# Norm statistics of two blocks on ScalarE, one head group moved forward, and the second GLU chunk's weights read and split early

## The chip, the cores and the metric

The kernel runs on one core of a Trainium2 chip. The metric is the device time of one execution in microseconds (us), the median of several runs. TensorE (PE) multiplies, VectorE (DVE) and ScalarE (ACT) do the elementwise work, GpSimd (POOL) does small operations and some DMAs, SyncE (SP) only issues DMAs. Each engine runs its instructions in order; they wait for one another through semaphores.

## The reference, cut to what matters

One transformer layer over 2048 tokens of width 576: a layernorm, sliding attention (32 heads of 18, eight keys each, two tokens apart), an output projection with a residual, a second layernorm, and a GLU of hidden width 4608 with a second residual.

```python
def _layernorm(x, axis=-1, eps=1e-5):
    m = jnp.mean(x, axis=axis, keepdims=True)
    v = jnp.var(x, axis=axis, keepdims=True)
    return (x - m) / jnp.sqrt(v + eps)
...
idx = pos[:, None] - off[None, :]          # off = 0, 2, ..., 14
...
logits = jnp.einsum("bhsd,bhswd->bhsw", q, kg) * scale
logits = jnp.where(mask[None, None, :, :], logits, -1e9)
attn = _softmax(logits, axis=-1)
o = jnp.einsum("bhsw,bhswd->bhsd", attn, vg)
...
h = x + _A_ref(_layernorm(x, axis=-1), A_wqkv, A_wo)
h2 = h + _B_ref(_layernorm(h, axis=-1), ...)   # (sigmoid(x Wg) * (x Wu)) Wd
```

Everything is float32. Products on PE are made from numbers split into a high part, rounded to PE's format, and the low rest, as three products: high times high, low times high, high times low.

## The kernel before

**Blocks.** The tokens are split by parity and by half into four blocks (0 to 3) of 512 tokens, each four tiles (j) of 128 tokens. The 32 heads are four groups (g) of eight. "(b, g)" below is block b, head group g.

**The stage before the GLU.** `ln1` normalises a block: for each tile `ln_j` makes the norm, PE transposes the result (`tr_main`, `tr_rest`), and `split` makes high and low parts: a Copy on ACT gives the high part, a subtraction on DVE the low one. In `ln_j` the mean and the variance come from DVE (`bn_stats` twice, `bn_aggr`, an add of eps), the power -0.5 from POOL. For blocks 0 and 1 (`on_act` false) DVE also subtracts and scales; for blocks 2 and 3 (`on_act` true) DVE negates the mean and ACT subtracts it (L130), scales (L131) and copies 64 columns (L132).

`qkv(b, g)` makes four projection tiles of 14 matmuls each over 432 columns (`tok_major`, L150 to L153), ACT evicts each one (L384) and ACT's queue stores q, k and v to DRAM. `attention(b, g)` loads q and two overlapping windows of k and v, and does the products and sums on DVE: L182 and L186 twice (logits), the softmax with its exponential on ACT (L196), then L208, L214, L216 twice and L219 (the weighted sum). Three buffers hold the windows kw and vw. Block 0's results go to the tile o in SBUF; the others' are stored to DRAM by POOL (L221).

`att_all` goes through the attention of blocks 0 and 1 in a list of (b, g) written out by hand (L401). When (0, 3) is done, four copies (L409) complete o, and `ready` is set. `step` advances this generator a few yields at a time beside the projections, so that their trace orders interleave. A scheduler then orders each engine's instructions by their place in the trace, moved ahead by `tc.high_priority(n)`, and by when their inputs and memory are expected.

`front` projects block 0's o (`proj_j`: transposes, eight groups of 14 matmuls over 288 columns, residual, `ln_j`, transposes, splits) and leaves X["a00"] and X["a01"], the transposed normed input of the GLU's first items, in two tiles of the pool xt. It also stores h (L503) and the transposed norm ar, which lies in a tile named tok (L505, "x<-tok" in the trace).

**The change of stage.** The weights of GLU chunk 0 are loaded into a tile of xt (L539) and split there (`first_split`). After that the pools of the attention stage are closed (L543, L544), and the GLU's pools (gw, gh, gd, gc, st) take the same memory; a tile of these waits until what lay there has been read, stores included. Chunk 1 is loaded into gw by POOL's queue (L565 through L979), and the down weights of chunk 0 are split into a tile d of gd (L980, L981).

**The GLU.** `items` are handled in order: 14 "std" items for block 0, then others that take two blocks. A std item makes two products of 14 matmuls over 512 columns (`single`: `prod` L609, `rest` L616), a sigmoid on ACT (L653), the gate on DVE (L629) and the split of the hidden tile. Every second item queues its down products (`down_std`, L723, L733). At the start of item c the weights of item c + 1 are split (`weights`) and those of item c + 2 loaded (`load_gu`, SP). In the background (`under_first`) run the rest of the attention of block 1, a load of the projection weights (`wos_early`, from item 3 on) and, from item 6 on, the projection of block 1 (`proj_scr`, which reads the attention's results back as oj).

The slots that matter here: xt has three "th" and four "tl" slots, shared by the operands of the blocks, wg0, the split weights of chunk 0 (wf), the early projection weights and the operands of the GLU; sah has two slots "h" for raw input and for the raw QKV weights of group 3.

Of the kernel before, what the change touches and what calls it, by code (L numbers as in the profile page):

```python
# [21 lines left out]
P = 128  # L22
S = 2048
D = 576
# [36 lines left out]
def kernel(ctx, tc, x, wqkv, wo, wmlp, out):  # L61
# [53 lines left out]
                sp.dma_start(bass.AP(tensor=a.tensor, offset=a.offset,  # L115
                                     ap=[[LP * CG // 16, 16], [1, LP * CG // 16]]), zero)

    def ln_j(xj, xn, on_act):
        bs = sm.tile([P, 2, 6], F32, bufs=4, name="bs")
        mv = sm.tile([P, 2], F32, bufs=4, name="mv")  # L120
        rstd = sm.tile([P, 1], F32, bufs=4, name="rstd")
        for k in range(2):
            dve.bn_stats(bs[:, k], xj[:, k * DH2:(k + 1) * DH2])
        dve.bn_aggr(mv, bs)
        dve.tensor_scalar(rstd, mv[:, 1:2], EPS, None, ALU.add)
        pool.tensor_tensor(rstd, rstd, mhalf, ALU.pow)
        if on_act:
            nm = sm.tile([P, 1], F32, bufs=4, name="nm")
            dve.tensor_scalar(nm, mv[:, 0:1], -1.0, None, ALU.mult)
            act.activation(xn[:, :D], xj, AF.Identity, bias=nm)  # L130
            act.activation(xn[:, :D], xn[:, :D], AF.Copy, scale=rstd)  # L131
            act.activation(xn[:, D:DX], xn[:, DM:D], AF.Copy)  # L132
        else:
            dve.tensor_scalar(xn[:, :D], xj, mv[:, 0:1], rstd, ALU.subtract, ALU.mult)
            dve.tensor_copy(xn[:, D:DX], xn[:, DM:D])

    def tr_main(ps, xn):
        for c in range(4):
# [86 lines left out]
    def step(gen, n):  # L225
        for _ in range(n):
            if next(gen, END) is END:
                return
# [11 lines left out]
    def proj_j(bank, t, wos, th, tl, xn_tile, put, order=(0, 1)):  # L240
        oj = t[0]
        pv = tr_main(bank(), oj)
        with tc.high_priority(HI):
            split(th[:, 0:4], tl, pv)
        yield
        pv = tr_rest(bank(), oj)
        with tc.high_priority(HI):
            split_rest(th[:, 4], pv)
        yield
        for i in order:  # L250
            ps = bank()
            tok_major(ps, DH2, th, tl, slice(0, P), *wos[i])
            hs = t[1][:, i * DH2:(i + 1) * DH2]
            with tc.high_priority(HI):
                dve.tensor_tensor(hs, hs, ps[:, :DH2], ALU.add)
            yield
        xn = xn_tile()
        with tc.high_priority(HI):
            ln_j(t[1], xn, False)
# [62 lines left out]
    def tok_tile(shape=(P, NS, DX)):  # L322
        return stk.tile(list(shape), F32, tag="tok", bufs=2, name="tok")
# [14 lines left out]
    def ln1(b, xb):  # L338
        th = th3_tile(F32R) if b == 3 else th_tile()
        tl = tl_tile()  # L340
        yield th, tl
        xn = tok_tile()
        for j in range(NS):
            js = slice(j * P, (j + 1) * P)
            pri = 2 * HI if b == 0 else HI if b > 1 else 0
            with tc.high_priority(pri):
                ln_j(xb[:, j], xn[:, j], b > 1)
            pv = tr_main(mm_tile(), xn[:, j])
            pr = tr_rest(acc_tile(), xn[:, j])
            with tc.high_priority(pri):  # L350
                split(th[:, 0:4, js], tl[:, :, js], pv)
                split_rest(th[:, 4, js], pr)
            yield
# [44 lines left out]

    def att_all():
        nonlocal o  # L400
        for b, g in ((0, 0), (0, 1), (1, 0), (0, 2), (0, 3), (1, 1), (1, 2), (1, 3)):  # L401
            while (b, g) not in emitted:
                yield
            if o is None:
                o = tok_tile()
            yield from attention(at, b, g, None if b else o[:, :, g * CG:(g + 1) * CG])
            if (b, g) == (0, 3):
                for j in range(NS):
                    dve.tensor_copy(o[:, j, D:DX], o[:, j, DM:D])  # L409
                ready.append(b)  # L410
# [108 lines left out]
    fr = front()  # L519
    for _ in qkv(1, 3, T[1], w[3]):  # L520
        step(ag, 1 if ready else 4)
    while not ready:
        step(ag, 1)
    more = qkv(2, 3, T[2], w[3])
# [15 lines left out]
                ww = first_split(wg)  # L540
    with tc.high_priority(HI):
        drain(fr)
    ps_stk.close()  # L543
    sa_stk.close()  # L544

# [342 lines left out]
    def under_first():  # L888
        wos = [None, None]
        for _ in ag:  # L890
            if c >= 3 and wos[1] is None:
                wos[1] = wos_early()
            yield ATT
        at_stk.close()
        a1 = xt.tile([P, 5, TB], F32, tag="th", bufs=3, name="ar")
        with sb_pool("pj", "right") as pj:
# [78 lines left out]
    items = ([("std", 0, f) for f in range(NSTD)] + [("pair", 0, f) for f in range(NSTD, NF)]  # L975
             + [("std", 1, f) for f in range(NSTD)] + [("pair", 1, f) for f in range(NF)])
    bg = under_first()
    with tc.high_priority(2 * HI):
        wg2 = load_gu(1, pool)  # L979
        d = d_tile()  # L980
        split(d[:, 0], d[:, 1], wg[:, GU:WC])  # L981
        wc = ww, d
    wg = wg2
    seg = []

    def last_pair(i):
# [123 lines left out]
    for c, (kind, p, f) in enumerate(items):  # L1110
# [11 lines left out]
        if c == NF + NSTD:  # L1122
# [4 lines left out]
            X = Xn  # L1127
            pp_stk.close()
            dw = ctx.enter_context(sb_pool("dw", "right"))
        if c + 1 < len(items):  # L1130
            wc = weights(items[c + 1][0], wg, c + 1 < NF + NSTD)
        if c + 2 < len(items):
            wg = load_gu(items[c + 2][2], n=WC if c + 2 < NF + NSTD else GU)
# [94 lines left out]
```

## Time and profile before

| | |
|---|---|
| runs | 1588.43 us median of 3 (1588.12 to 1588.75) |
| profiled execution | its span, 1589.2 us, first to last instruction; the page gives no other time of it |
| mean granted clock of TensorE | 0.993 |
| matmuls | 8532 |
| DMA | 273.50 MB, mean 172 GB/s |

In the rows quoted below, a time such as "120.00 2.50" is the start and the length in us from the span's start; "out<-in" are tiles by the program's names, "xN" is the number of instructions merged into the row, and "[8.68 <-DMA x<-tok]" is idle time of the engine just before it and what ended it. ACTq, SPq and POOLq are DMA issues. A line such as L104 or L105 can be that of a helper (`split`), so the tile names tell which use it is. Group rows give the count, the busy us in total and the mean ns of one, then the idle time ahead. In rows of windows each engine's busy us stands with its count, then the granted clock (1.00 is full speed), the DMA share and GB/s. A matmul's length includes filling and draining the array, so consecutive ones overlap and the start-to-start time is the one that adds up.

### The profile page before, as it was taken

How to read it: one execution, taken by the hardware profiler on the slowest of the kernel's cores; microseconds unless marked ns; L12 is line 12 of the kernel's file. 1: busy time of each engine (PE TensorE's matmuls, PEld its weight loads, DVE VectorE, ACT ScalarE, POOL GpSimd, SP SyncE). 2: the span in 40 equal slices, each digit the busy share in tenths (PEclk: the TensorE clock that was granted, in tenths of full speed). 3: DMA queues.
4: the chain of work that ended last, by engine and by line, in shares of the span. 5: the costliest groups of instructions: out<-in, count | busy, mean ns of one | idle time of the engine just before them, and what ended most of it. 6: DMA issues, size and time to landing. Idle time of an engine off the chain costs nothing.

```text
span 1589.2 us, 22383 instructions
## 1 busy us (share of the span) xinstructions
PE 1553.3 (98%) x8532; PEld 1381.6 (87%) x8532; DVE 1268.1 (80%) x1931; ACT 869.2 (55%) x1546; POOL 184.2 (12%) x230
## 2 busy tenths in 40 slices
PE   7999979999999999999989999999999999999998
PEld 6999968888888888888879988888888888888887
DVE  7999988959999999999546687876677776677755
ACT  4432234425555666656443255776677776677761
POOL 1000000011010001000101100122112112212210
PEclk9999999999999999999999999999999999999999
DMA  7664544346367565665764234899989999989983
GB/s 267 208 206 163 193 184 165 133 177 246 104 164 205 157 170 139 166 191 149 210 203 143 100 110 110 182 186 181 176 169 183 184 173 180 177 170 182 184 170 124
DMA packets 76892, 273.50 MB, mean 172 GB/s; under 512 B 8336, under 2 KB 14224, under 8 KB 75888
## 3 DMA queue, kind: packets, MB, share of 16 engines
q0 software_dynamic: 27792, 105.89, 36.3%
q1 hardware_dynamic: 41360, 146.06, 27.4%
q10 hardware_dynamic: 7632, 20.12, 3.3%
q8 instruction: 67, 1.10, 0.3%
q14 instruction: 41, 0.34, 0.1%
HBM read 145.88 MB, written 128.52 MB: 173 GB/s over the span
## 4 chain that ended last, share of the span: by engine, by line
PE 55%; issue 27%; POOL 7%; DVE 6%; DMA 4%; ACT 1%; SPq 0%; POOLq 0%; ACTq 0%; DVEq 0%
PE b L609 23%; PE dp L723 15%; POOL h L794 7%; PE acc L150 6%; PE b L616 4%; PE b L150 1%; PE bgp L150 1%; DMA wg<-in_wmlp_dram 1%; DVE pr L182 1%; DMA x<-tok 1%; DVE pr L208 1%; DVE lg L186 1%; PE acc L152 1%; DMA tail<-h 1%; PE acc L153 1%
## 5 line engine op out<-in xcount | busy, mean ns | idle before, releaser
L609 PE MATMUL b<-tl,w 128*128 128x512 f32 x1716 | 438.1, 395 | 9.1 <-ACT w L104 6.5
L609 PEld LDWEIGHTS b<-tl,w 128*128 128x128 f32 x1716 | 311.7, 189 | 66.5 <-ACT w L104 7.7
L609 PE MATMUL b<-th,w 128*128 128x512 f32 x1368 | 352.8, 393 | 0.4 <-DVE s L698 0.3
L609 PEld LDWEIGHTS b<-th,w 128*128 128x128 f32 x1368 | 249.8, 188 | 46.7 <-DVE s L698 0.7
L104 ACT ACTIVATE w<-wg 128x640 fp32r<-128x640 f32 (+2 forms) x197 | 117.0, 598 | 125.2 <-PE b L616 59.8
L791 ACT ACTIVATE ev<-dp 128x576 f32<-128x576 f32 x224 | 145.0, 647 | 61.8 <-PE dp L785 58.2
L616 PE MATMUL b<-th,w 128*128 128x512 f32 x572 | 177.0, 391 | 0.0
L794 POOL DMA_DIRECT2D h<-ev x128 | 110.2, 862 | 456.8 <-ACT ev L791 440.5
L105 DVE TENSOR_TENSOR w<-wg,w 128x640 fp32r<-128x640 f32 (+2 forms) x197 | 126.8, 649 | 38.7 <-ACT w L104 38.3
L150 PE MATMUL acc<-qw,th 128*128 128x432 f32 x512 | 155.7, 365 | 1.2 <-DVE th L109 0.9
L105 DVE TENSOR_TENSOR w<-tw,w 128x512 fp32r<-128x512 f32 x116 | 79.6, 687 | 81.1 <-ACT w L104 80.2
L616 PEld LDWEIGHTS b<-th,w 128*128 128x128 f32 x572 | 107.7, 188 | 23.1
L723 PE MATMUL dp<-d,h0h 128*128 128x288 f32 x640 | 119.0, 296 | 1.7 <-DVE tail L733 1.7
L723 PE MATMUL dp<-d,h1h 128*128 128x288 f32 x640 | 120.0, 297 | 0.0
L723 PEld LDWEIGHTS dp<-d,h0h 128*128 128x128 f32 x640 | 99.4, 189 | 5.5 <-DVE tail L733 2.0
L150 PEld LDWEIGHTS acc<-qw,th 128*128 128x128 f32 x512 | 97.2, 190 | 6.5 <-DVE th L109 1.1
L723 PEld LDWEIGHTS dp<-d,h1h 128*128 128x128 f32 x640 | 99.5, 190 | 2.9
L731 ACT ACTIVATE stage<-dp 128x576 f32<-128x576 f32 x96 | 61.7, 646 | 62.4 <-PE dp L723 62.3
L104 ACT ACTIVATE w<-tw 128x512 fp32r<-128x512 f32 x116 | 72.8, 628 | 41.3 <-PE b L609 40.9
L150 PE MATMUL acc<-qw,tl 128*128 128x432 f32 x256 | 92.8, 362 | 0.0
L384 ACT ACTIVATE ev<-acc 128x432 f32<-128x432 f32 x64 | 33.9, 531 | 104.4 <-PE acc L153 97.7
L182 DVE TENSOR_TENSOR pr<-kw,q 128x2304 f32<-128x2304 f32 x32 | 81.7, 2552 | 2.8 <-DMA kw<-k 2.6
(278 smaller groups left out, 2899.8 us busy)
## 6 DMA issues: line engine op xcount, KB each, us to landing
h<-ev POOLq DMA_DIRECT2D x96, 576.0 KB, 7.2
wg<-in_wmlp_dram SPq DMA_DIRECT2D x49, 928.0 KB, 5.2
h<-stage POOLq DMA_DIRECT2D x24, 1152.0 KB, 10.6
wg<-in_wmlp_dram SPq DMA_DIRECT2D x36, 640.0 KB, 4.1
kw<-k SPq DMA_DIRECT2D x16, 792.0 KB, 4.4
vw<-v SPq DMA_DIRECT2D x16, 792.0 KB, 5.5
wd<-in_wmlp_dram SPq DMA_DIRECT2D x18, 576.0 KB, 7.2
h<-ev POOLq DMA_DIRECT2D x32, 288.0 KB, 6.8
```

The source lines that it names most:

```text
L104: act.activation(hi, src, AF.Copy)
L105: splits.append(dve.tensor_tensor(lo, src, f32(hi), ALU.subtract))
L150: pe.matmul(ps[:, :n], a[:, c, js], m[:, c], start=k == 0, stop=False)
L152: pe.matmul(ps[:, :n], th[:, 4, js], wh[:, 4], start=False, stop=False)
L182: dve.tensor_tensor(pr, both(kw, u), q[:, us].unsqueeze(2).broadcast_to([P, 2, W, CG]), ALU.mult)
L384: act.activation(ev[:, :, j], ps[:, :NQ].rearrange("p (t c) -> p t c", t=3), AF.Copy)
L609: pe.matmul(ps, wt[:, a, k0 + c], xx[:, m + c], start=first and k == 0, stop=k == 5, skip_group_check=True)
L616: pe.matmul(ps, wt[:, a, k0], xx[:, 4], start=False, stop=a == 1, skip_group_check=True)
L723: pe.matmul(ps[:, i, :DH2], a[:, js], d[:, m, i * DH2:(i + 1) * DH2], start=k == 0, stop=k == n)
L731: act.activation(hv, ps, AF.Copy)
L791: act.activation(hs[:, k % 2], ps[:, :, :DH2], AF.Copy)
L794: pool.dma_start(hsev[:, u, k0:k + 1], hs[:, :k + 1 - k0], accum_op=ALU.add, max_dma_last_dim=8 * D)
```

## The change

1. `ln_j` keeps only the DVE form. For blocks 2 and 3, `ln_stats` makes the statistics on ACT: a Copy scaled by -1/D with a sum (the negative mean), an Identity with that as bias, a Square with a sum (the variance, its elementwise output written over the raw input). POOL adds eps and takes the power. `ln_scale` then scales and copies on ACT. `ln1` issues the statistics two tiles ahead at first, then one tile ahead of the scaling.
2. In `att_all` (1, 1) stands ahead of (0, 3).
3. The raw weights of GLU chunk 1 are loaded by SP into a slot "h" of sah, before front; they are split into a second wf tile, and the down weights of chunks 0 and 1 into tiles df in "tl" slots, all before the pools close. POOL's load and the first d tile are gone; item 1 takes its weights from there.
4. `under_first` waits for item 3 before it loads the projection weights, also where the attention is through earlier.

```diff
-    def ln_j(xj, xn, on_act):
+    def ln_j(xj, xn):
...
-        if on_act:
-            nm = sm.tile([P, 1], F32, bufs=4, name="nm")
-            dve.tensor_scalar(nm, mv[:, 0:1], -1.0, None, ALU.mult)
-            act.activation(xn[:, :D], xj, AF.Identity, bias=nm)
-            act.activation(xn[:, :D], xn[:, :D], AF.Copy, scale=rstd)
-            act.activation(xn[:, D:DX], xn[:, DM:D], AF.Copy)
-        else:
-            dve.tensor_scalar(xn[:, :D], xj, mv[:, 0:1], rstd, ALU.subtract, ALU.mult)
-            dve.tensor_copy(xn[:, D:DX], xn[:, DM:D])
+        dve.tensor_scalar(xn[:, :D], xj, mv[:, 0:1], rstd, ALU.subtract, ALU.mult)
+        dve.tensor_copy(xn[:, D:DX], xn[:, DM:D])
+
+    def ln_stats(xj, xn):
+        mv = sm.tile([P, 2], F32, bufs=4, name="mv")
+        nm, var = mv[:, 0:1], mv[:, 1:2]
+        rstd = sm.tile([P, 1], F32, bufs=4, name="rstd")
+        act.activation(xn[:, :D], xj, AF.Copy, scale=-1.0 / D, accum_out=nm)
+        act.activation(xn[:, :D], xj, AF.Identity, bias=nm)
+        act.activation(xj, xn[:, :D], AF.Square, scale=D ** -0.5, accum_out=var)
+        pool.tensor_scalar(rstd, var, EPS, None, ALU.add)
+        pool.tensor_tensor(rstd, rstd, mhalf, ALU.pow)
+        return rstd
+
+    def ln_scale(rstd, xn):
+        act.activation(xn[:, :D], xn[:, :D], AF.Copy, scale=rstd)
+        act.activation(xn[:, D:DX], xn[:, DM:D], AF.Copy)
...
+        def stats(n):
+            with tc.high_priority(pri):
+                for j in range(len(rstd), n):
+                    rstd.append(ln_stats(xb[:, j], xn[:, j]))
...
+            if b > 1:
+                stats(min(j + 2, NS))
             with tc.high_priority(pri):
-                ln_j(xb[:, j], xn[:, j], b > 1)
+                if b > 1:
+                    ln_scale(rstd[j], xn[:, j])
+                else:
+                    ln_j(xb[:, j], xn[:, j])
...
-        for b, g in ((0, 0), (0, 1), (1, 0), (0, 2), (0, 3), (1, 1), (1, 2), (1, 3)):
+        for b, g in ((0, 0), (0, 1), (1, 0), (0, 2), (1, 1), (0, 3), (1, 2), (1, 3)):
...
     for _ in qkv(1, 3, T[1], w[3]):
         step(ag, 1 if ready else 4)
+    with tc.high_priority(HI):
+        wg1 = sah.tile([P, NS, D], F32, bufs=2, name="h").rearrange("p j d -> p (j d)")[:, :WC]
+        sp.dma_start(wg1, wmlp[1])
...
+    def first_down(ws):
+        d = xt.tile([P, 2, D], F32R, tag="tl", bufs=4, name="df")
+        split(d[:, 0], d[:, 1], ws[:, GU:WC])
+        return d
+
+    with tc.high_priority(HI):
+        wc = ww, first_down(wg)
+        wc_next = first_split(wg1), first_down(wg1)
...
             if c >= 3 and wos[1] is None:
                 wos[1] = wos_early()
             yield ATT
+        while c < 3:
+            yield ATT
+        if wos[1] is None:
+            wos[1] = wos_early()
...
-    with tc.high_priority(2 * HI):
-        wg2 = load_gu(1, pool)
-        d = d_tile()
-        split(d[:, 0], d[:, 1], wg[:, GU:WC])
-        wc = ww, d
-    wg = wg2
...
-        if c + 1 < len(items):
+        if c == 0:
+            wc = wc_next
+        elif c + 1 < len(items):
             wc = weights(items[c + 1][0], wg, c + 1 < NF + NSTD)
```

More of the change, by code (lines that the diff above doesn't have):

```diff
@@ L258, in proj_j @@
         with tc.high_priority(HI):
-            ln_j(t[1], xn, False)
+            ln_j(t[1], xn)
         yield
@@ L342, in ln1 @@
         xn = tok_tile()
+        pri = 2 * HI if b == 0 else HI if b > 1 else 0
+        rstd = []
+        def stats(n):
+            with tc.high_priority(pri):
+                for j in range(len(rstd), n):
+                    rstd.append(ln_stats(xb[:, j], xn[:, j]))
         for j in range(NS):
             js = slice(j * P, (j + 1) * P)
-            pri = 2 * HI if b == 0 else HI if b > 1 else 0
+            if b > 1:
+                stats(min(j + 2, NS))
             with tc.high_priority(pri):
-                ln_j(xb[:, j], xn[:, j], b > 1)
+                if b > 1:
+                    ln_scale(rstd[j], xn[:, j])
+                else:
+                    ln_j(xb[:, j], xn[:, j])
             pv = tr_main(mm_tile(), xn[:, j])
```

## The prediction

> **What bounds the kernel now.** I read the page first, then the busy time by stretches of 20 us, then the order of instructions in the stretch where TensorE is least busy, and last the chain of waits around it.
>
> ```profile
> span 1589.2 us, 22383 instructions
> PE 1553.3 (98%) x8532; PEld 1381.6 (87%) x8532; DVE 1268.1 (80%) x1931; ACT 869.2 (55%) x1546; POOL 184.2 (12%) x230
> ```
>
> TensorE (PE) is busy for 98% of the span, so a change can win only what PE loses: gaps, and time at a lower clock. The stretches show where that is. The columns after the window are PE, weight loads, VectorE (DVE), ScalarE (ACT), GpSimd (POOL), the granted clock and the DMA share.
>
> ```profile
> 20.00:40.00 20.00, 20.00 (x111) 18.95 (x110) 15.51 (x52) 11.46 (x27) 4.27 (x8) 1.00 0.87 303
> 40.00:60.00 20.00, 18.88 (x109) 17.42 (x108) 19.44 (x40) 13.77 (x32) 2.20 (x4) 1.00 0.75 253
> ...
> 180.00:200.00 20.00, 18.67 (x127) 18.06 (x126) 19.80 (x30) 5.17 (x13) 0.00 (x0) 1.00 0.56 198
> 200.00:220.00 20.00, 19.22 (x119) 17.49 (x117) 18.61 (x44) 7.82 (x22) 2.41 (x4) 1.00 0.27 104
> 220.00:240.00 20.00, 10.86 (x45) 8.58 (x46) 15.46 (x13) 7.84 (x17) 1.33 (x2) 0.81 0.70 260
> ...
> 300.00:320.00 20.00, 17.60 (x101) 15.50 (x100) 15.85 (x22) 7.61 (x13) 1.45 (x2) 1.00 0.47 154
> ```
>
> The worst stretch is 220 to 240, where the GLU begins: 9.1 us of gap and a clock of 0.81. Its instructions:
>
> ```profile
> 221.19 0.33 ACTq L505 DMA_DIRECT2D x<-tok  x1
> ...
> 224.78 0.57 POOL L565 DMA_DIRECT2D wg<-in_wmlp_dram  x1
> ...
> 228.89 0.61 PE L616 MATMUL b<-th,wf 128*128 128x512 f32 x2
> 232.36 0.68 ACT L104 ACTIVATE d<-wg 128x576 fp32r<-128x576 f32 x1 [8.68 <-DMA x<-tok]
> ...
> 235.24 2.08 ACT L104 ACTIVATE w<-wg 128x640 fp32r<-128x640 f32 x4 [0.29 <-DMA wg<-in_wmlp_dram]
> ...
> 236.03 1.22 PE L609 MATMUL b<-tl,w 128*128 128x512 f32 x2 [6.52 <-ACT w L104]
> ...
> 242.69 2.77 PE L609 MATMUL b<-th,w 128*128 128x512 f32 x6
> ...
> 246.97 1.54 PE L609 MATMUL b<-th,w 128*128 128x512 f32 x6
> ```
>
> ACT stands for 8.68 us at the first down-weight split, because the tile d lies where the store of x (the transposed norm, issued at 221.19) still reads; it lands at 232.36, 11.1 us later. Behind it in ACT's order are the sigmoid of item 0 and the weight splits of item 1, whose weights POOL only asked for at 224.78 and which came at 235.24. PE ends item 0 at 229.5 and stands for 6.52 us. Two causes end within 3 us of each other, so both have to go. After the gap six matmuls take 2.77 us instead of 1.54: half speed.
>
> ```profile
> 232.30:245.95 13.65, 7.41 (x17) 5.52 (x18) 11.59 (x13) 6.42 (x10) 0.00 (x0) 0.50 0.36 125
> ...
> 321.04:324.45 3.41, 3.41 (x15) 3.10 (x14) 2.05 (x3) 0.74 (x3) 0.00 (x0) 0.50 1.04 417
> ```
>
> By 245.95 PE has done the 28 matmuls of item 0 (24 products and 4 rests by the code) and 17 more. At 0.23 us each (1.54 less the 0.39 that one takes alone, over 5) that is 10.3 us, so the GLU runs **as if it had begun at 235.7 and never stopped**. That is the number to beat. Later there is one more loss:
>
> ```profile
> PE b L139 <- DMA oj<-o: 2.4, 1, 2.4
> ```
>
> 2.4 us in the stretch 300 to 320, where block 1's projection waits for attention that DVE finishes late, and 1.7 us (half of 3.41) at clock 0.50 behind it: 4.1 us.
>
> **Part 1, statistics of blocks 2 and 3 to ACT.** DVE loses eight sets of bn_stats, aggregate, add and negate. Block 3's four sets, from the groups between 36 and 48 us, and the attention that waits meanwhile:
>
> ```profile
> L123 DVE BATCH_NORM_STATS2 bs<-h 128x6 f32<-128x288 f32 x8 | 3.3, 434 | 0.0
> ...
> L124 DVE BATCH_NORM_AGGREGATE mv<-bs 128x2 f32<-128x12 f32 x4 | 0.8, 201 | 0.0
> L129 DVE TENSOR_SCALAR nm<-mv 128x1 f32<-128x1 f32 x4 | 0.6, 144 | 0.0
> L125 DVE TENSOR_SCALAR rstd<-mv 128x1 f32<-128x1 f32 x4 | 0.6, 138 | 0.0
> ```
> ```profile
> 35.95 2.56 DVE L182 TENSOR_TENSOR pr<-kw,q 128x2304 f32<-128x2304 f32 x1 [2.58 <-DMA kw<-k]
> ```
>
> The sum is 5.3 us; neighbours overlap a little, so I take 4.5, with 0 and 5.3 as ends. Block 2's four sets run before 35.95, when the attention waits for its keys anyway: worth nothing. From there DVE is nearly full (19.44 of 20, and 19.80 at 180 to 200), so the 4.5 us arrive at everything that follows on it. ACT gains two passes over 576 columns for each of eight tiles. Neither a Copy nor a Square with a sum is in this trace; the nearest rows are
>
> ```profile
> L130 ACT ACTIVATE tok<-h,nm 128x576 f32<-128x576 f32 x8 | 5.9, 772 | 0.0
> L126 POOL TENSOR_TENSOR rstd<-rstd,mhalf 128x1 f32<-128x1 f32 x12 | 6.5, 562 | 30.5 <-DVE rstd L125 19.3 <-DVE nm L129 9.8 <-DVE mv L124 1.4
> ```
>
> so 16 x 0.77 = 12.3 us at the low end; twice that if writing out the sum cost a pass of its own; I take 13. ACT has 8.5 us free in 20 to 40 and 6.2 in 40 to 60, 14.8 together, and can begin without DVE, so the pass is hidden, just. If it isn't, block 3's operands are late, and evictions of the QKV tiles queue behind statistics on ACT: up to 12 us of ACT, less the tiles that PE has to do meanwhile. POOL's added eps step is at most 0.56 us a tile, off ACT's path because the statistics run a tile ahead of the scaling.
>
> **Part 2, (1,1) ahead of (0,3).** Front, that is block 0's output projection, second norm and transposes, needs (0,3). One attention on DVE:
>
> ```profile
> 130.72 2.55 DVE L182 TENSOR_TENSOR pr<-kw,q 128x2304 f32<-128x2304 f32 x1
> ...
> 143.91 0.67 DVE L198 TENSOR_REDUCE rs<-lg 128x32 f32<-128x256 f32 x1 [1.25 <-ACT lg L196]
> ...
> 155.69 2.55 DVE L182 TENSOR_TENSOR pr<-kw,q 128x2304 f32<-128x2304 f32 x1
> ...
> 180.86 0.76 DVE L219 TENSOR_TENSOR tok<-kw 128x576 f32<-128x576 f32 x1
> ...
> 184.00 0.49 DVE L409 COPY tok<-tok 128x64 f32<-128x64 f32 x4
> ```
>
> 25.0 us from 130.72 to 155.69, of which 1.25 waited for the exponential where 0.5 is usual: 24.2. So (0,3) ends at 181.6 + 24.2 - 4.5 = 201.3, and o is complete 2.9 us after, as 184.5 stands to 181.6: **204.2 instead of 184.5**. What did PE do beside front? QKV tiles:
>
> ```profile
> 101.72 2.34 PE acc L150 x12
> 104.45 2.36 PE acc L150 x12
> ```
> ```profile
> L153 PE MATMUL acc<-qw,th x7: 352/358/360, 183.8 to 222.8; 128*128 128x432 f32 x7
> ```
>
> A tile takes 2.73 us. The first of these seven ends at 184.2; six are left, 16.4 us, so without front PE is through with QKV at **200.6**. From there it has front alone, and starves 3.6 us. Front's own length:
>
> ```profile
> 189.85 1.59 PE mm L150 x12
> ...
> 191.71 1.59 PE mm L150 x12
> ```
> ```profile
> 217.42 2.55 DVE L208 TENSOR_TENSOR pr<-vw,lg 128x2304 f32<-128x2304 f32 x1
> ...
> 220.00 0.71 DVE L109 TENSOR_TENSOR th<-acc,th 64x128 fp32r<-64x128 f32 x3
> ```
>
> From o (184.5) to the last operand (220.7) are 36.2 us. One QKV tile that stood among the projections (2.7) is gone, and so is a 2.55 us attention step that stood right ahead of the last splits, because their transposes no longer queue behind QKV: 31.0. The last operand is read by the 13th matmul only (12 x 0.23 = 2.8), so the GLU runs as if begun 28.2 us after o: 204.2 + 28.2 = 232.4. In those 28 us PE has only 8 groups of 1.86, 14.9 us, and a few transposes.
>
> Gaps halve the clock. The trace grants 0.50 for 3.41 us behind a wait of 2.4, and for 13.65 behind 6.52. I charge two stretches of 3.41 at half, one as the projections begin and one as the GLU begins: 2 x 1.7 = 3.4; ends 0 and 8.5 (1.7, and half of 13.65). The Trainium skill, "TensorE: Matmul & The Clock Gate", Part 1, says that the array falls to half its clock after one idle window of about 3.4 us and needs a busy one to come back. By that alone the starving of 3.6 us could miss a full window and the sum would be 1.7 better; the row at 321.04 shows the halving after only 2.4 us, and I go by the row.
>
> **Part 3, the early weights.** wg1 goes through SP into a half of the tile h that is free after the last QKV weight split, off POOL's queue at 224.78; its splits and both d tiles lie in slots of the operand pool, so neither the store of x nor the load stands before item 1. Both causes of the 6.52 us are gone. The splits are the same instructions as before, only earlier, in front's gaps. What is late next: the third item's d is the first in the old place, and its ACT split now waits for the store, with the sigmoid of item 1 and later splits behind it. With the load gone I take that store nearer to this one (the other of like size), not to 11.1:
>
> ```profile
> h<-h ACTq DMA_DIRECT2D x1, 1152.0 KB, 5.2
> ```
>
> That is over before item 0 is through; I charge 0.5, ends 0 and 5.5. On SP the early projection weights now wait until the two d tiles are read; weight loads queue behind, each an item ahead of need: 0.
>
> **The sum.** 232.4 + 3.4 + 0.5 = 236.3 against 235.7: the GLU starts **0.6 us later** in effect. After it DVE has one attention left, not two, so of the 4.1 us at 300 to 324 I expect 0.5 to stay: 3.6 won. Together -3.0 on the profiled 1589.2. The median of the runs is 1588.4, 0.8 lower, so the forecast is **1585.4**, 1581.5 to 1589 by the small terms.
>
> **The rivals.** (a) **Front is short.** If PE, freed of QKV, lets two more of the 2.55 us attention steps fall outside front (5.1), and the clock holds (3.4), the GLU gains 8.5 more: 1576.9. For it: DVE's order gives front precedence, and only steps that have started delay it. Against: the same attention, now (1,2), fills the same gaps. (b) **PE starves in front, slower.** Place: the 20 us between the end of QKV and the GLU. If front keeps its 36.2 us (DVE sets it, not PE), 5.2 are lost, and at the clock's far end 5.1 more: 1585.4 + 10.3 = 1595.7; half of the second gives 1593. It decides once front exceeds about 34 us. For it: DVE at 18.61 to 19.80 of 20 there; against: PE was full as well. (c) **It doesn't do what it says**: ACT again stands at the store of x, an item later, for the far end of 5.5: 1590.4. The DMA share of 0.70 beside it speaks for this, the missing 0.9 MB load against. (d) ACT's extra passes hold up block 3 and its evictions: some 5 us of PE, 1590 to 1600.
>
> **How the numbers follow.** The forecast has 0.40, (a) 0.22, (b) 0.25, (c) 0.08, (d) 0.05. A measurement of this kernel tells 0.2%, 3.2 us, from no change: the bound is 1585.3, so half of the forecast's 0.40 counts as faster, 0.18 as the same and 0.02 as slower. Faster 0.20 + 0.22 = 0.42; same 0.18 + 0.07 of (c) = 0.25; slower 0.02 + 0.25 + 0.01 + 0.05 = 0.33. Both signs hold much, so the range reaches from (a) to (b): 1576 to 1597; the forecast's own stands above.
>
> **What would show it.** Right: no bn_stats between 36 and 48; the copy L409 near 204; PE gaps between about 200 and 236 at a clock below 1; no wait of PE for ACT's w split and no store of x ahead of item 1; no wait for oj. Wrong: the copy later than 208, QKV still running beside front, ACT waiting several us on the store of x, or PE gaps between 40 and 70 where ACT carries the statistics.

## The result and the profile after

The changed kernel takes **1607.69 us** (median of 4 runs, 1606.01 to 1608.89) against 1588.59 for the kernel before in the same job (4 runs, 1588.12 to 1589.09). The ratio is 1.0118, 95% interval 1.0103 to 1.0132: slower by 19.1 us, where 1585.4 was forecast and 1597 was the upper end. The first lines of its page, and its busy time by stretches of 20 us (columns as before: PE, weight loads, DVE, ACT, POOL, granted clock, DMA share, GB/s):

```profile
span 1607.0 us, 22376 instructions
...
PE 1555.3 (97%) x8532; PEld 1384.5 (86%) x8532; DVE 1263.6 (79%) x1891; ACT 877.7 (55%) x1576; POOL 186.9 (12%) x237
```
```profile
40.00:60.00 20.00, 11.15 (x50) 9.93 (x49) 14.51 (x16) 12.95 (x33) 4.82 (x8) 0.74 0.51 178
60.00:80.00 20.00, 16.45 (x84) 14.63 (x83) 14.39 (x18) 12.76 (x33) 1.58 (x4) 0.91 0.29 104
180.00:200.00 20.00, 20.00 (x103) 19.07 (x102) 19.79 (x16) 5.72 (x12) 0.73 (x1) 1.00 0.58 215
200.00:220.00 20.00, 2.59 (x17) 1.94 (x15) 19.07 (x19) 3.01 (x6) 0.00 (x0) 0.62 0.41 161
220.00:240.00 20.00, 19.27 (x123) 19.18 (x124) 18.84 (x29) 3.21 (x9) 0.00 (x0) 0.86 0.00 1
240.00:260.00 20.00, 19.04 (x106) 16.93 (x105) 18.98 (x46) 10.04 (x28) 3.19 (x5) 1.00 0.62 212
300.00:320.00 20.00, 20.00 (x110) 17.58 (x109) 15.49 (x24) 8.22 (x15) 1.45 (x2) 1.00 0.48 166
```

Two holes are new, at 40 to 80 and at 200 to 220. The old hole at 220 to 240 (10.86 busy, clock 0.81) is filled (the 0.86 there is the rest of the half clock behind the new hole), and so is the one at 300 to 320. PE's waits, summed by what ended them (us in total, times, longest):

```profile
PE mm L147 <- DVE tok L227: 14.1, 1, 14.1
...
PE acc L158 <- ACT th L104: 6.5, 2, 5.9
PE mm L147 <- DVE tl L105: 5.9, 4, 2.9
PE acc L151 <- DVE tok L429: 4.1, 1, 4.1
```

Gaps and half clock together are easiest counted as **lost time**: the length of a stretch less what the matmuls that start in it need at full rate (0.11 us for a transpose, 0.133 for 288 columns, which is 1.86 / 14, 0.195 for 432, which is 2.73 / 14, and 0.229 for 512). All kernels here run the same 8532 matmuls, some 1538 us by that count, so a difference in lost time is a difference in span. The four rates are rounded, which can move an entry by 0.2 us.

| PE's lost time, us | 20 to 80 | 180 to 260 | 280 to 340 |
|---|---|---|---|
| before | 1.6 | 16.2 | 5.6 |
| after | 17.9 | 22.9 | -0.1 |
| difference | +16.3 | +6.7 | -5.7 |

The three sum to +17.3, of the 17.8 by which the spans differ.

**The early hole.** What PE waits for at 46 us is the high part of block 1's first tile: the eight QKV tiles of (0, 0) and (0, 1) are done, and the ninth, of (1, 0), is the first that reads block 1. Before, ACT made this split at 38.57, behind its work for block 2's norm:

```profile
30.78 1.44 ACT L130 ACTIVATE tok<-h,nm 128x576 f32<-128x576 f32 x2
...
38.28 0.39 ACT L132 ACTIVATE tok<-tok 128x64 f32<-128x64 f32 x2
38.57 0.59 ACT L104 ACTIVATE th<-mm 128x512 fp32r<-128x512 f32 x1
```

After, on ACT and on PE:

```profile
32.49 0.78 ACT L142 ACTIVATE tok<-tok,rstd 128x576 f32<-128x576 f32 x1 [0.42 <-POOL rstd L138]
...
41.98 0.78 ACT L142 ACTIVATE tok<-tok,rstd 128x576 f32<-128x576 f32 x1 [2.50 <-POOL rstd L138]
...
45.46 0.58 ACT L104 ACTIVATE th<-mm 128x512 fp32r<-128x512 f32 x1
```
```profile
30.01 0.60 PE L147 MATMUL mm<-ident,tok 128*128 128x128 f32 x4
...
46.09 0.73 PE L158 MATMUL acc<-qw,th 128*128 128x432 f32 x1 [5.91 <-ACT th L104]
...
49.76 1.11 PE L147 MATMUL mm<-ident,tok 128*128 128x128 f32 x4 [2.95 <-DVE tl L105]
```

PE transposed this tile at 30.01, before ACT scaled any tile of block 2 (the first at 32.49), and yet its split starts at 45.46, 6.9 us later than before. `ln1` gives block 2's norm `tc.high_priority(HI)` and block 1's splits none, in both kernels. Before, that did no harm: the split at 38.57 was in time for PE, which came to (1, 0) at 40.51. Now the statistics of all four tiles of block 2 and three of its four scalings stand ahead of block 1's split in ACT's order, with a wait of 2.50 us for POOL at 41.98. The 2.95 us at 49.76 follow from it: block 1's fourth tile is transposed into one of three buffers `mm`, all held by its tiles that wait for their splits.

VectorE, which was to gain, loses too. The reciprocal of the first attention's softmax stands at 62.28 in the kernel before and at 71.72 after:

```profile
62.28 0.35 DVE L199 RECIPROCAL rs<-rs 128x32 f32<-128x32 f32 x1
```
```profile
71.72 0.35 DVE L207 RECIPROCAL rs<-rs 128x32 f32<-128x32 f32 x1
```

Of these 9.4 us, 2.7 are there when the attention starts (38.66 instead of 35.95): SP now loads block 3's input ahead of its keys. After that DVE waits for high parts that ACT makes late: 9.5 us between 20 and 75, where it was 0.7 before.

**The hole at 200.** PE's instructions, and the group of the last QKV matmuls with its first and last start:

```profile
200.66 0.82 PE L147 MATMUL acc<-ident,tok 128*128 128x128 f32 x6
215.55 0.69 PE L147 MATMUL mm<-ident,tok 128*128 128x128 f32 x2 [14.07 <-DVE tok L227]
...
220.73 0.87 PE L151 MATMUL acc<-ident,tok 128*128 128x128 f32 x3 [4.06 <-DVE tok L429]
```
```profile
L161 PE MATMUL acc<-qw,th x16: 353/358/443, 175.1 to 258.3; 128*128 128x432 f32 x16
```

The transposes of o stand in PE's order ahead of QKV tiles that run up to 258.3. They wait 14.07 us for the last step of (0,3) and 4.06 for the copies, and nothing behind them can run. The same transposes then open front, on DVE from the copies to the last split:

```profile
214.74 0.76 DVE L227 TENSOR_TENSOR tok<-kw 128x576 f32<-128x576 f32 x1
...
220.40 0.49 DVE L429 COPY tok<-tok 128x64 f32<-128x64 f32 x4
...
255.68 0.71 DVE L109 TENSOR_TENSOR th<-acc,th 64x128 fp32r<-64x128 f32 x3
```

From the end of the copies (220.9) to the end of the last split (256.4) are 35.5 us, where 31.0 were forecast and 36.2 measured before.

### The profile page after: what moved, and what is told of

Read it like the earlier page. It is cut to its first block, busy times and chain, and to the rows that moved or that the text cites. A ratio compares the mean times of both kernels' runs of the same rounds, so it can differ in the third digit from the quotient of the medians.

```text
span 1607.0 us, 22376 instructions
## 1 busy us (share of the span) xinstructions
PE 1555.3 (97%) x8532; PEld 1384.5 (86%) x8532; DVE 1263.6 (79%) x1891; ACT 877.7 (55%) x1576; POOL 186.9 (12%) x237
## 3 DMA queue, kind: packets, MB, share of 16 engines
q0 software_dynamic: 27648, 104.94, 35.5%
## 4 chain that ended last, share of the span: by engine, by line
PE 86%; DVE 8%; DMA 2%; ACT 1%; issue 1%; POOL 0%; SPq 0%; ACTq 0%; DVEq 0%; POOLq 0%
PE b L641 43%; PE dp L755 15%; PE dp L817 11%; PE b L648 8%; PE acc L158 4%; DVE pr L190 1%; DVE lg L194 1%; PE b L158 1%; PE bgp L158 1%; DVE pr L216 1%; DMA wg<-in_wmlp_dram 1%; DVE pr L222 1%; DVE tl L105 1%; DMA tail<-h 0%; PE b L147 0%
## 5 line engine op out<-in xcount | busy, mean ns | idle before, releaser
L641 PE MATMUL b<-tl,w 128*128 128x512 f32 x1704 | 431.7, 393 | 0.0
L641 PEld LDWEIGHTS b<-tl,w 128*128 128x128 f32 x1704 | 308.3, 188 | 55.4 <-DVE s L661 0.3
L641 PEld LDWEIGHTS b<-th,w 128*128 128x128 f32 x1356 | 246.7, 188 | 45.6 <-DVE s L661 0.5
L104 ACT ACTIVATE w<-wg 128x384 fp32r<-128x384 f32 (+2 forms) x194 | 115.4, 598 | 116.8 <-PE b L648 61.5
L105 DVE TENSOR_TENSOR w<-wg,w 128x384 fp32r<-128x384 f32 (+2 forms) x194 | 124.9, 649 | 36.2 <-ACT w L104 28.4
L648 PEld LDWEIGHTS b<-th,w 128*128 128x128 f32 x568 | 106.7, 188 | 23.3
L755 PE MATMUL dp<-d,h0h 128*128 128x288 f32 x608 | 112.5, 295 | 1.5 <-DVE tail L765 1.5
L755 PEld LDWEIGHTS dp<-d,h0h 128*128 128x128 f32 x608 | 93.6, 189 | 4.5 <-DVE tail L765 1.7
```

Of the source, the lines that this page charges most:

```text
L104: act.activation(hi, src, AF.Copy)
L105: splits.append(dve.tensor_tensor(lo, src, f32(hi), ALU.subtract))
L641: pe.matmul(ps, wt[:, a, k0 + c], xx[:, m + c], start=first and k == 0, stop=k == 5, skip_group_check=True)
L648: pe.matmul(ps, wt[:, a, k0], xx[:, 4], start=False, stop=a == 1, skip_group_check=True)
L755: pe.matmul(ps[:, i, :DH2], a[:, js], d[:, m, i * DH2:(i + 1) * DH2], start=k == 0, stop=k == n)
```

## The experiments

First the parts one by one and in pairs (statistics with order, without the weights, was not run), each timed in 3 rounds beside the kernel before (its median 1590.4 in the first job, 1590.1 in the second, which had statistics with weights). The first, fourth and fifth edit are shown against the changed kernel, the second and third against the kernel before.

**Early weights alone** (parts 3 and 4 kept; statistics and order as before):

```diff
+                ln_j(xb[:, j], xn[:, j], b > 1)
...
-        for b, g in ((0, 0), (0, 1), (1, 0), (0, 2), (1, 1), (0, 3), (1, 2), (1, 3)):
+        for b, g in ((0, 0), (0, 1), (1, 0), (0, 2), (0, 3), (1, 1), (1, 2), (1, 3)):
```

> Part 3 alone on the kernel before. Theory A (both causes of the stall at the start of the GLU are gone with it, and nothing else moves): TensorE loses about 10 of the 12.9 us between 229 and 246 no more, 1577 to 1581 us. Rival (the store of x only blocks ScalarE an item later, or the late attention of block 1 takes the gain back at its projection): 1585 us or more, with a wait of several us of ScalarE for the store or of TensorE for oj.

**Statistics alone** (the kernel before with the new `ln_j`, `ln_stats`, `ln_scale` and `ln1`):

```diff
-                ln_j(xb[:, j], xn[:, j], b > 1)
+                if b > 1:
+                    ln_scale(rstd[j], xn[:, j])
```

> Part 1 alone. Theory A (the loss of 16 us that the trace of after shows between 20 and 80 us comes from the statistics on ScalarE alone): TensorE idles in the same place, 1600 to 1606 us. Rival (it needs the other parts, or the later stages absorb it because DVE is ahead): 1586 to 1592 us.

**Order alone** (the kernel before with the new list in `att_all`, and the new wait for item 3 in `under_first`):

```diff
-        for b, g in ((0, 0), (0, 1), (1, 0), (0, 2), (0, 3), (1, 1), (1, 2), (1, 3)):
+        for b, g in ((0, 0), (0, 1), (1, 0), (0, 2), (1, 1), (0, 3), (1, 2), (1, 3)):
```

> Part 2 alone. Theory A (block 0's projection comes one attention, some 24 us, later, TensorE has nothing ready for a part of it, and the old stall still follows): 1594 to 1602 us. Rival (the QKV tiles still fill the time, so the order costs nothing): 1587 to 1590 us.

**Order and early weights** (the changed kernel with the old `ln_j` in all blocks):

```diff
-                if b > 1:
-                    ln_scale(rstd[j], xn[:, j])
+                ln_j(xb[:, j], xn[:, j], b > 1)
```

> Parts 2 and 3, statistics as before. Theory A (the order gives up in front of block 0's projection about what the early weights win): 1586 to 1594 us, no loss between 20 and 80 us. Rival (the early loss was of the order, not of the statistics): 1603 us or more.

**Statistics and early weights** (the changed kernel with the old list in `att_all`):

```diff
-        for b, g in ((0, 0), (0, 1), (1, 0), (0, 2), (1, 1), (0, 3), (1, 2), (1, 3)):
+        for b, g in ((0, 0), (0, 1), (1, 0), (0, 2), (0, 3), (1, 1), (1, 2), (1, 3)):
```

> Statistics and early weights together, attention in the old order; it completes the set of single parts and pairs. The theory (ScalarE's four statistics of a block stand ahead of the first operand split, PE loses some 16 us between 20 and 80 us, and nothing later takes that back while front keeps its place) expects the 15 us of the statistics alone over the early weights alone: 1582.5 + 15 = 1597, 1594 to 1600, PE waits for the th split in 40 to 70 as in the changed kernel. The rival (the loss is only visible where the GLU's start stalls, and early weights hide it) expects 1590 or less.

| kernel | median us (range) | ratio to before, interval | lost 20 to 80 | 180 to 260 | 280 to 340 |
|---|---|---|---|---|---|
| early weights | 1582.48 (1582.06 to 1584.88) | 0.9947 (0.9930 to 0.9963) | 2.1 | 10.1 | 3.0 |
| statistics | 1605.45 (1603.13 to 1605.94) | 1.0089 (1.0071 to 1.0107) | 18.1 | 12.0 | 4.4 |
| order | 1609.68 (1608.26 to 1611.43) | 1.0115 (1.0099 to 1.0132) | 2.1 | 33.6 | -0.2 |
| order, weights | 1596.98 (1595.36 to 1597.95) | 1.0037 (1.0022 to 1.0053) | 2.1 | 28.2 | 0.0 |
| statistics, weights | 1598.94 (1597.25 to 1602.52) | 1.0064 (1.0049 to 1.0080) | 16.6 | 10.3 | 1.7 |
| all (the change) | 1607.69 (1606.01 to 1608.89) | 1.0118 (1.0103 to 1.0132) | 17.9 | 22.9 | -0.1 |

Each part acts mainly on one stretch. On the kernel before, the statistics cost 15.1 us and the order 19.3, and the early weights win 7.9; only the last was worth having. The order came out dearer than expected both times (1594 to 1602 and 1586 to 1594); alone it also loses 5 us at 260 to 280, where the old stall of the GLU's start now lies. Beside the weights, the statistics cost 16.5, the order 14.5, and both together 25.2: a PE that is late at 80 waits less at 200 (28.2 lost there without the statistics, 22.9 with them).

The early weights alone come out 1.5 us above the expected range, and they show what is late next. PE waits 4.4 us for item 0's gate, which stands on DVE behind two products and reductions of the attention:

```profile
236.39 2.42 PE L621 MATMUL b<-tl,wf 128*128 128x512 f32 x6 [4.40 <-DVE s L641]
```
```profile
233.07 2.54 DVE L186 TENSOR_REDUCE lg<-pr 128x128 f32<-128x2304 f32 x1
235.65 0.69 DVE L641 TENSOR_TENSOR s<-s,b 128x512 f32<-128x512 f32 x1
```

**Which block's statistics cost, and is it their place or their amount?** Early weights, old order, with block 3 alone or block 2 alone on ScalarE:

```diff
-            if b > 1:
+            if b == 3:
                 stats(min(j + 2, NS))
```

> Early weights, old order, and the ScalarE statistics for block 3 only. The theory that it is the place in ScalarE's order that costs (block 2 is the one PE waits for at 46 us; block 3 has PE work of block 2 beside it) expects most of the 16 us to be gone: 1584 to 1589. The rival, that it is the amount of ScalarE work in 20 to 80, expects half of it: about 1590 and more.

```diff
-            if b > 1:
+            if b == 2:
                 stats(min(j + 2, NS))
```

> As the run before with block 2 in place of block 3. Place in the order: 1590 to 1597, PE's waits for th and tl at 46 to 50 us as in the changed kernel. Amount of work: about 1590, the same as with block 3 alone.

and block 2 alone with its statistics tied behind the split of the tile ahead (`hs` collects the ACT half of `split`):

```diff
-            if b == 2:
+            if b == 2 and j:
+                with tc.issue_after(getattr(hs[-1], "ins", hs[-1])):
+                    stats(min(j + 2, NS))
+            elif b == 2:
-                stats(min(j + 2, NS))
+                stats(2)
```

> Early weights, old order, statistics of block 2 on ScalarE, each tile's statistics behind the first operand split of the tile two ahead of it on ScalarE, where they stood ahead of the first split of all. Same instructions, another order. The theory that the place in ScalarE's order costs expects most of the 11 us (1593.6 against 1582.5) back: 1583 to 1587, and no wait of PE over 3 us for th between 40 and 60. The rival, that the amount of ScalarE work costs (seven more microseconds until the last split), expects 1589 or more.

| kernel | median us (range) | ratio to before, interval | lost 20 to 80 | 180 to 260 |
|---|---|---|---|---|
| block 3 on ACT | 1583.81 (1580.39 to 1584.57) | 0.9961 (0.9948 to 0.9974) | 1.4 | 11.0 |
| block 2 on ACT | 1593.58 (1592.43 to 1595.73) | 1.0025 (1.0014 to 1.0036) | 12.5 | 11.6 |
| block 2, tile by tile | 1588.00 (1585.59 to 1589.93) | 0.9989 (0.9980 to 0.9998) | 2.9 | 15.2 |

The stretch 40 to 60 of the three, in this order:

```profile
40.00:60.00 20.00, 19.28 (x112) 18.03 (x110) 16.94 (x23) 16.78 (x43) 2.38 (x6) 1.00 0.54 184
```
```profile
40.00:60.00 20.00, 10.23 (x49) 9.34 (x50) 16.00 (x29) 12.39 (x31) 5.11 (x6) 0.74 0.59 190
```
```profile
40.00:60.00 20.00, 17.82 (x100) 15.98 (x99) 18.28 (x33) 14.63 (x36) 4.12 (x8) 1.00 0.67 224
```

ACT is busiest where PE loses nothing (16.78 of 20 with block 3), so the amount in the stretch is not what decides. Block 3's statistics start at 44.44, behind block 1's four splits (from 37.92 on); block 2's stand ahead of them. With the same instructions in another order block 1's first split starts at 34.44 instead of 44.28 (first the order as changed, then tile by tile), PE loses 2.9 instead of 12.5 in 20 to 80, and place explains block 2's early loss:

```profile
44.28 0.58 ACT L104 ACTIVATE th<-mm 128x512 fp32r<-128x512 f32 x1
```
```profile
34.44 0.59 ACT L105 ACTIVATE th<-mm 128x512 fp32r<-128x512 f32 x1
```

The time came back by half only (5.6 of 11.1), between the two expectations. The rest moved to 190, where the transposes of o now wait for the copies, since on DVE an attention step and splits stand between; DVE reaches (0,3)'s end 6 us later than with the weights alone, although it has less to do. Over half of that is there at its first product (39.17 instead of 35.78), whose keys SP loads at 33.19 instead of 29.88, behind block 3's input:

```profile
192.20 0.88 PE L159 MATMUL acc<-ident,tok 128*128 128x128 f32 x3 [3.98 <-DVE tok L440]
```

**Is it PE's order at front, or VectorE?** Four edits of the kernel with order and early weights (1596.98). First, all QKV tiles issued ahead of front:

```diff
-    for _ in range(2):
-        next(more)
-        step(ag, 1)
...
     for b in (2, 3):
         for _ in more if b == 2 else qkv(b, 3, T[b], w[3]):
-            next(fr, END)
             step(ag, 1)
...
+    last = passes[-1]
+    with tc.issue_after(getattr(last, "ins", last)):
+        for _ in range(2):
+            next(fr)
```

> New order and early weights, with all QKV tiles of blocks 2 and 3 issued ahead of front on every engine, so that PE has them to do while DVE finishes (0,3). The theory (PE stood 19.5 and 4.1 us because it takes its instructions in order and the transposes of o stand ahead of some six QKV tiles of 2.73 us, 16.4 in all) expects those tiles to fill the wait of 19.5 and the clock to stay up: 1597.0 less 6 to 16, thus 1581 to 1591, with no wait over 8 us for the attention output. The rival (VectorE paces front, PE's order matters little, the tiles only change places) expects 1594 to 1599.

Then the attention (1,2) kept behind front on VectorE (`held` gets the last split of front):

```diff
+            if (b, g) == (1, 2):
+                while not held:
+                    yield
+                while True:
+                    with tc.issue_after(getattr(held[0], "ins", held[0])):
+                        if next(ga, END) is END:
+                            break
+                    yield
```

> New order and early weights, with the attention (1,2) queued on VectorE behind front's last operand split, so that none of its steps stands in front. The theory (VectorE paces front: from the copies of o to the last split it took 36.7 us before, 35.6 in this kernel's parent and 33.4 with QKV out of PE's way, and some 19 of them were attention steps of another head group) expects front of 25 us or less, bound by the six QKV tiles and front's own 15 us of PE: the GLU starts 6 to 9 us earlier and 4 us more are won because the step between the end of (0,3) and the copies is gone; VectorE has 24 us more to do under the GLU. 1597.0 less 6 to 13: 1584 to 1591. The rival (front is a chain of hand-overs between PE, ScalarE and VectorE, and needs its 33 us without the attention too) expects 1594 or more.

then both of these edits:

> Both of the former at once: all QKV tiles ahead of front, and the attention (1,2) behind it, so that PE has the tiles to do while VectorE finishes (0,3) and VectorE has front alone after it. The theory by now: whatever PE does first, it has some 31 us of work (QKV tiles 16.4, front 15) for the time from 184 to the GLU's start, and that start cannot come before the end of (0,3), at 204 to 211, plus front's own length; QKV first left it the attention as company (33.4 us), front alone left it the QKV tiles (36 us from the copies at 204). Without either, front should take 22 to 26 us and the GLU start at 228 to 236: 1599.9 less 6 to 12, thus 1588 to 1594, still above the early weights alone in the old order (1582.5), since there PE has the tiles as well as front to do. The rival (front is a chain of hand-overs of over 30 us whatever stands beside it) expects 1597 or more.

and both, with the splits of chunk 0's weights behind the copies that complete o (their load moves behind the QKV tiles, too):

```diff
-            with tc.high_priority(2 * HI):
-                wg = xt.tile([P, WC], F32, tag="tl", bufs=4, name="wg0")
-                sp.dma_start(wg, wmlp[0])
-                ww = first_split(wg)
...
+    with tc.issue_after(getattr(ready[0], "ins", ready[0])):
+        with tc.high_priority(HI):
+            ww = first_split(wg)
```

> As the run with both (QKV tiles ahead of front, attention (1,2) behind it), and the splits of GLU chunk 0's weights put behind the copies that complete o, so that (0,3) should end at about 205 again, not at 211. If the end of (0,3) plus front's own 30 us sets the GLU's start, that start comes 6 us earlier: 1595.3 less 5 to 7, 1588 to 1590. If PE's total wait is what counts, and it only moves, 1594 to 1597.

| kernel | median us (range) | ratio to before, interval | (0,3) ends | front, us | lost 180 to 260 |
|---|---|---|---|---|---|
| order, weights | 1596.98 (1595.36 to 1597.95) | 1.0037 (1.0022 to 1.0053) | 204.7 | 35.6 | 28.2 |
| QKV first | 1599.88 (1596.39 to 1600.48) | 1.0060 (1.0043 to 1.0077) | 211.2 | 33.4 | 30.1 |
| front alone | 1596.64 (1595.78 to 1597.38) | 1.0046 (1.0029 to 1.0063) | 204.3 | 37.1 | 26.2 |
| both | 1595.25 (1592.00 to 1597.08) | 1.0031 (1.0016 to 1.0045) | 211.1 | 29.8 | 22.7 |
| both, splits later | 1591.86 (1588.48 to 1592.61) | 1.0007 (0.9998 to 1.0016) | 205.5 | 31.5 | 18.5 |

("Front" is from the start of the copies to the end of the last operand split on DVE.) In the kernel that they start from, PE waits longest at the same transposes:

```profile
204.77 0.69 PE L139 MATMUL mm<-ident,tok 128*128 128x128 f32 x2 [19.50 <-DVE tok L219]
```

With the tiles first PE runs to 201 without a gap, and the wait is 9.27 us, then 4.06 for the copies:

```profile
211.21 0.69 PE L139 MATMUL mm<-ident,tok 128*128 128x128 f32 x2 [9.27 <-DVE tok L219]
...
216.39 0.88 PE L143 MATMUL acc<-ident,tok 128*128 128x128 f32 x3 [4.06 <-DVE tok L409]
```

and the time is no better, though not by the order alone: (0,3) itself ended 6.5 us later here, behind weight splits on DVE that waited for ACT. Front alone doesn't help either. With both, DVE is no longer full, and PE isn't:

```profile
220.00:240.00 20.00, 12.97 (x87) 11.58 (x85) 14.11 (x43) 8.04 (x23) 2.79 (x4) 0.87 0.32 113
```

Front by itself is a chain of hand-overs of some 30 us (22 to 26 were expected), with about 15 us of PE in it. Put the QKV tiles before it, and front is short but starves; put them beside it, and PE has work, but has stood 19.5 us before. What all five share is that (0,3) ends at 204 at the earliest and that PE has 31 us of work from 184 on (16.4 of QKV tiles, 15 of front), which cannot fill the time to 204 plus 30. Taking the late splits away (the last row) let (0,3) end 5.6 us earlier and gave 3.4 us, less than the 5 to 7 expected, as front grew by 1.7: that end sets most of the time, not all. Even so the new order loses 9.4 us against the early weights alone. The theory that PE's blocked order is the cause fell: mended, along with front's company, it is worth 5.1 us (1596.98 to 1591.86) of the 14.5 that the order costs beside early weights. How the 5.1 divide stays open, as the QKV tiles first without the late splits were not run by themselves.

**The gate first.** To the early weights alone, in the old order: the second product and reduction behind item 0's gate.

```diff
     def twice(i):
+        if c == 0:
+            if i == 4:
+                with tc.issue_after(getattr(gate[0], "ins", gate[0])):
+                    for _ in range(4):
+                        bg_step(i)
+            if i > 1:
+                return
         bg_step(i)
```

> Early weights alone, and on VectorE the second product and its reduction of the attention put behind the first gate of the GLU, which PE waited for 4.4 us at 236. If that wait and the half clock behind it (3.4 us at half, 1.7) are lost time: 1582.5 less 4 to 6, 1576 to 1579. If VectorE is what bounds until the attention is through: the 5 us come back at 300 to 320 as a longer wait for oj, 1581 to 1584.

**1575.67 us** (1574.58 to 1577.31), ratio 0.9913 (0.9898 to 0.9928): the fastest kernel of the study, 14 us under the kernel before. The gate now stands ahead of the product, and the stretch is full:

```profile
231.69 0.69 DVE L643 TENSOR_TENSOR s<-s,b 128x512 f32<-128x512 f32 x1
232.29 2.55 DVE L182 TENSOR_TENSOR pr<-kw,q 128x2304 f32<-128x2304 f32 x1
```
```profile
220.00:240.00 20.00, 19.72 (x92) 16.59 (x90) 19.87 (x22) 10.72 (x22) 0.76 (x1) 1.00 0.69 261
```

PE loses 5.2 us in 180 to 260 instead of 10.1, and the attention that was put off doesn't come back as a wait (1.4 lost in 280 to 340).

**Can the statistics pay at all?** That kernel with the statistics of both blocks on ScalarE, tile by tile:

```diff
-            if b > 1:
-                stats(min(j + 2, NS))
+            if b > 1 and j:
+                with tc.issue_after(getattr(hs[-1], "ins", hs[-1])):
+                    stats(min(j + 2, NS))
+            elif b > 1:
+                stats(2)
```

> The fastest version so far (early weights, old order, first gate ahead of the attention; 1575.7) with the statistics of blocks 2 and 3 on ScalarE, tile by tile. If a VectorE that is freed of 4.5 us still brings something: 1571 to 1575. If VectorE no longer sets the time once the weights are early and the gate is first, or if the splits that wait for ScalarE take back on VectorE what the statistics freed: 1576 to 1582.

1591.62 us (1586.66 to 1593.22), ratio 1.0006 (0.9996 to 1.0016), 16 above its parent and far over both expectations. The order that mended block 2 doesn't mend two blocks: PE again loses 13.9 us in 20 to 80 (2.1 with the early weights alone); the other few are spread over later stages. Now it waits for the scaling of blocks 2 and 3, and DVE for an exponential that stands behind statistics on ACT:

```profile
63.09 1.12 PE L148 MATMUL mm<-ident,tok 128*128 128x128 f32 x4 [4.38 <-ACT tok L143]
```
```profile
64.19 0.63 DVE L207 TENSOR_REDUCE rs<-lg 128x32 f32<-128x256 f32 x1 [6.95 <-ACT lg L205]
```

So place is not the whole of it. Each tile adds a loop from ACT to POOL and back, and whichever of ACT's other duties (splits, evictions, exponentials) is queued behind it comes late; moving it only chooses which. How much of the 13.9 belongs to each stays open.

## Why the prediction was wrong, step by step

- **Part 1, the price of ACT's passes: right.** 0.68 us with a sum and 0.19 for its read-out, which overlap by 0.1, are the 0.77 that was taken for a pass.
- **Part 1, "so the pass is hidden, just": this step failed**, and it is the larger error, 16.3 us where 0 stood. The 14.8 us that ACT had free in 20 to 60 were compared with 13 us of work, but a sum of free time says nothing of what the work stands in front of. Block 2's statistics stood ahead of block 1's first split, which PE needed next and which was in time by less than 2 us before. The prediction looked for late operands of block 3 only. Its rival (d) had the mechanism, for block 3, at 5 us and a chance of 0.05; block 3 alone cost 1.3 us, which the intervals don't tell from nothing, and block 2, whose removal from DVE had been called worth nothing, cost 11.1.
- **Part 1, POOL "off ACT's path": failed.** ACT waited 4.4 us for it in 20 to 75, 2.5 of them behind the lengthened step of the last section.
- **Part 1, DVE relieved of 4.5 us: wrong in sign.** The statistics did leave it, but DVE came to the first softmax 9.4 us later: its own splits wait for ACT's, and its keys came later.
- **Part 2, the end of (0,3): right in the one attention, wrong in the time.** One attention more was to cost 24.2 us; with the old statistics and early weights (0,3) ended at 204.7 instead of 181.6, 23.1 later. In the changed kernel it ended at 215.5, not 201.3: 10.8 more came from the early delay, where 4.5 less were counted. And o was complete 5.4 us behind it, not 2.9, since an attention step and four splits stood ahead of the copies: 220.9 instead of 204.2.
- **Part 2, PE through with QKV at 200.6 and starving for 3.6 us: failed.** Where the tiles do go first they end at 200.5, as worked out. In the changed kernel they stand behind the waiting transposes of o, and PE stood 14.1 and 4.1 us. The runs show that this choice decides little: with the tiles first, front starves later.
- **Part 2, front in 31.0 us: mis-sized**, 35.5 in the changed kernel. About 30 us are reached only without QKV tiles and without attention beside it, and a front of that kind starves PE. Rival (b) was this, "if front keeps its 36.2 us", with 0.25. Against the early weights alone the order added 18.1 us of lost time in 180 to 260; with all parts it was 6.7 more than before. The GLU begins at 258.5 and doesn't stall, where 236.3 was forecast and 235.7 the number to beat; the early hole is the larger share of that.
- **The clock: about as charged in this place.** One long stretch at 0.50, of 20.5 us from 205.0, took the place of the two of 3.4, but most of it lay in the waits. PE worked in some 5.5 us of it, so the half clock cost about 2.7 us, where 3.4 were charged.
- **Part 3: right.** No PE wait for w is left and no store of x stands before item 1; alone it gave 8 us. What came late next was not the third item's down weights (0.5 forecast) but the gate behind the attention, 4.4 us, hidden in the full change because the attention is elsewhere.
- **Later, 3.6 us won: right in kind**, 5.7 by lost time; PE waits for oj no more.

The sum was +0.6 - 3.6 = -3.0 and came out as 16.3 + 6.7 - 5.7 = +17.3. Both errors went the same way, which is why the time lies beyond the upper end.

## What to carry to other kernels

Free time on an engine is no cover until you know what the new work stands in front of in that engine's order: ask which instruction follows it, who waits for that, and whether that one is full. Moving a task ahead of the one that opens the next stage delays that stage by the task's whole length, and the engine that waits needs that much other work. When a change has several parts, build each alone: here one was worth 8 us (14 with the gate moved), and it lay under two that cost 15 and 19 by themselves.

## What the runs showed of the hardware

**A small GpSimd operation waits out a large VectorE one.** The added eps step takes 0.22 us, but in the changed kernel 2.54 where it began just behind a product of two SBUF operands on DVE:

```profile
36.27 0.22 POOL L137 TENSOR_SCALAR rstd<-mv 128x1 f32<-128x1 f32 x1 [3.81 <-ACT h L136]
...
38.76 2.54 POOL L137 TENSOR_SCALAR rstd<-mv 128x1 f32<-128x1 f32 x1 [1.62 <-ACT h L136]
```
```profile
38.66 2.56 DVE L190 TENSOR_TENSOR pr<-kw,q 128x2304 f32<-128x2304 f32 x1 [8.74 <-DMA kw<-k]
```

It ends at 41.30, 0.08 behind the product, and ACT's scaling at 41.98 waited 2.50 us for it and for the power behind it. With block 2 alone on ACT the power of -0.5 ran under a reduction, which has one input, at its usual length:

```profile
47.00 0.57 POOL L145 TENSOR_TENSOR rstd<-rstd,mhalf 128x1 f32<-128x1 f32 x1
```
```profile
46.87 2.55 DVE L201 TENSOR_REDUCE lg<-pr 128x128 f32<-128x2304 f32 x1
```

The prediction had this step at 0.56 us at most. The Trainium skill, "SBUF — State Buffer", "Who interferes with whom", says that a VectorE instruction with two SBUF inputs contends with a GpSimd instruction that reads SBUF, because its second input comes through the read interface that they share, and that a reduction never does on this chip. The two cases agree with it.
